# A fused attention, soft-MoE and SwiGLU kernel: the first SwiGLU units reordered, and weight conversion left out of iterations that end a pass

## The chip, the cores and the metric

One core of a Trainium2 chip runs the whole kernel. The time is device microseconds of one execution; of several executions the median is given. The engines are named as in the profile: PE (TensorE, matrix products; PEld is its weight load), DVE (VectorE), ACT (ScalarE), POOL (GpSimd), SP (SyncE, which issues the transfers here).

## The reference

Three layers follow each other on 4608 tokens of 512 features. The attention works in chunks of 64 tokens. The soft mixture of experts forms 32 slots from all tokens, sends each through its expert and mixes the slots back with a softmax `c` (one row of 32 weights for each token). The SwiGLU then is:

```python
g = x @ w_gate                    # w_gate, w_val: 512 x 1536, float64
silu = g * (1.0 / (1.0 + np.exp(-g)))
val = x @ w_val
out = (silu * val) @ w_out        # w_out: 1536 x 512, float64
```

The weights of the SwiGLU arrive as float64 and have to become float32 pairs on the chip.

## The kernel before, in words

**Stages.** Attention runs to about 128 us of the span, the experts to about 169 us, the SwiGLU from there to the end. Weights stream in through one queue (SP), in the order of the list `lq` (L128 to L138), as far as free slots of the pool `wp` allow.

**SwiGLU.** As `x` is `c` times the 32 slot outputs, the kernel multiplies the slot outputs with the gate and value weights first (`emit_g0` for chunk 0, L813; `emit_g` for the others, L822) and gets a small matrix `g_st`. For a block `b` of 512 tokens and a tile `f` of 128 hidden features, a unit (b, f), `emit_gv` (L840) makes two products with `c_t` (L847), ACT takes silu of one (L850), DVE multiplies by the other (L851). The unit's result is split into a high and a low float32r part: ACT copies (`hi`, L859), POOL or DVE subtracts (`lo`, L860). `emit_out` (L866) multiplies both with the high and low part of `w_out`: 4 tiles of 128 tokens by three products (L891 to L893; the first unit by L882), added up in PSUM over the units of a pass. At the end of a pass the four sums are copied out by ACT (L902) and DVE (L900), or added to the earlier sums by DVE (L904).

**Passes.** `SCHED` (L29) lists passes over 1536/256 = 6 weight chunks: blocks 0 to 4 with chunk 0 (two units each), then blocks 5 to 8 with chunks 0 and 1 (four units each), and so on; `seq` (L915) is the list of the 108 units, each with marks for the first and the last unit of its block's pass. Chunk 1 is used first by unit 12, (5, 2).

**Conversion.** Each half of a chunk of one weight kind ("g", "v", "o") goes through four stages: `conv_a` (ACT L185, DVE L186 and L187), `conv_b` (ACT L194, DVE L195), `conv_c` (DVE L200, POOL L213), `conv_d` (the high part by ACT L234, or by DVE L236 where asked; the low part L239 by POOL and DVE in turns). `conv_step` (L249) runs one stage of each half that is under way, last stage first, and starts a new half if told. Below, o01 is the second half of chunk 0 of `w_out`, v11 the second half of chunk 1 of `w_val`. The slot product of chunk 0 uses another form of conversion that ends at stage c.

**Order of issue.** The order on every engine is the order of these calls, written out by hand: L776 to L791 end the experts (`sos` L781, `sot_ps` L786, `so_t` L790 and L791), L921 to L939 issue the first two units and o00 and o01, and the loop over n (L949) issues, for each n:

- at its top, `conv_until`, which runs conversion steps until gate and value weights of unit n's chunk are done, and `emit_g` if that chunk has not had it;
- `emit_gv` of unit n, `emit_hl` (high and low part) of unit n-1;
- one `conv_step`, which may start a half if fewer than `RATE * n + R0` (0.38 n + 7.4) of the 36 halves are started;
- `emit_out` of unit n-2, and `emit_g` of the next chunk if its weights are done.

PSUM holds five tiles for the sums and the small slot products (`ps_o`), and three for L847 and the rest (`ps_g`).

Of the kernel before, what the change touches and what calls it, by code (L numbers as in the profile page):

```python
# [10 lines left out]
I32 = mybir.dt.int32  # L11
# [22 lines left out]
def tile_attn_softmoe_swiglu(  # L34
# [12 lines left out]
    nc = tc.nc  # L47
# [44 lines left out]
    def load_raw(kind, c, pool):  # L92
        src = {"o": w_out, "g": w_gate, "v": w_val}[kind][c]
        t = pool.tile([128, 2048], I32, tag="w", name="raw")
        nc.sync.dma_start(out=t, in_=src.bitcast(I32))
        raw_t[kind, c] = t[:, 0:1024], t[:, 1024:2048]

    raw0 = {}
# [169 lines left out]
    with tc.manual_schedule():  # L268
# [507 lines left out]
        dummy = sm.tile([128, 1], F32, tag="dm", name="dm", bufs=1)  # L776
        nc.scalar.activation(out=dummy, in_=cbias, func=ACTF.Silu)

        sos = t2.tile([128, DM], F32, tag="hs", name="sos", bufs=1)
        for o in range(0, DM, DM // 2):  # L780
            nc.scalar.activation(  # L781
# [3 lines left out]
        for kk in range(4):  # L785
            nc.tensor.matmul(  # L786
                out=sot_ps[kk // 2][:, kk % 2], lhsT=sos[:, kk * 128:(kk + 1) * 128],
                rhs=sel_big.rearrange("p j s -> p (j s)"), start=True, stop=True,
            )
        nc.scalar.activation(out=so_t[:, 0:2, 0:96], in_=sot_ps[0][:, :, 0:96], func=ACTF.Copy)  # L790
        nc.vector.tensor_copy(out=so_t[:, 2:4, 0:96], in_=sot_ps[1][:, :, 0:96])  # L791
        pp.close()
        pq.close()
        pa.close()
        ps_o = ctx.enter_context(tc.tile_pool(name="ps_o", bufs=5, space=PSUM, reuse_waits="tile"))
        ps_g = ctx.enter_context(tc.tile_pool(name="ps_g", bufs=3, space=PSUM, reuse_waits="tile"))
        ht2 = ctx.enter_context(tc.tile_pool(name="ht2", bufs=3, side="right"))
# [6 lines left out]
                out=so_hl[:, :, 96:128], in0=so_t[:, :, 0:32], in1=so_hl[:, :, 0:32].bitcast(F32), op=ALU.subtract  # L804
            )


        cvp[0] = ctx.enter_context(tc.tile_pool(name="cv2", bufs=4, side="right"))
        def evac_g(ps, gst):
            nc.scalar.activation(out=gst, in_=ps, func=ACTF.Copy)  # L810
            nc.vector.tensor_tensor(out=gst[64:96], in0=ps[64:96], in1=gst[64:96].bitcast(F32), op=ALU.subtract)
# [25 lines left out]
        def cols(parts):  # L837
            return [slice(i * 512 // parts, (i + 1) * 512 // parts) for i in range(parts)]

        def emit_gv(b, f, parts=1):  # L840
            c, ff = f // 2, (f % 2) * 128
            gp = ps_g.tile([128, 512], F32, tag="g", name="g_ps")
            vp = ps_g.tile([128, 512], F32, tag="g", name="v_ps")
            s = ht2.tile([128, 512], F32, tag="s", name="s_sb", bufs=2)
            for ps, gi in ((gp, 0), (vp, 1)):
                for k in cols(parts):
                    nc.tensor.matmul(out=ps[:, k], lhsT=g_st[:, c, gi, ff:ff + 128], rhs=c_blk(b)[:, k],  # L847
                                     start=True, stop=True)
            for k in cols(parts):
                nc.scalar.activation(out=s[:, k], in_=gp[:, k], func=ACTF.Silu)  # L850
                nc.vector.tensor_tensor(out=s[:, k], in0=s[:, k], in1=vp[:, k], op=ALU.mult)  # L851
            s_t[b, f] = s

        def emit_hl(b, f, eng, parts=1):
            s = s_t.pop((b, f))
            hi = ht2.tile([128, 512], F32R, tag="hi", name="hi_sb")
            lo = ht2.tile([128, 512], F32R, tag="lo", name="lo_sb")
            for k in cols(parts):
                nc.scalar.activation(out=hi[:, k], in_=s[:, k], func=ACTF.Copy)  # L859
                eng.tensor_tensor(out=lo[:, k], in0=s[:, k], in1=hi[:, k].bitcast(F32), op=ALU.subtract)  # L860
            hl[b, f] = (hi, lo)

        acc_t = {}
        part = {}

        def emit_out(b, f, first, last, mid=None):  # L866
            hi, lo = hl.pop((b, f))
            c, ff = f // 2, f % 2
            w = w_split("o", c)
            w_hi, w_lo = w[:, ff, 0], w[:, ff, 1]  # L870
            done = f == NFT - 1
            if last and not done and b not in part:
                assert slots[0]
                slots[0] -= 1
                resv[0] -= 1
                part[b] = wp.tile([128, 4, DM], F32, tag="w", name="part"), True
            if mid:
                for i, (x, w) in enumerate(((hi, w_hi), (lo, w_hi), (hi, w_lo))):
                    for t in range(4):
                        if i == 0:  # L880
                            acc_t[t] = ps_o.tile([128, DM], F32, tag="o", name=f"o{t}")
                        nc.tensor.matmul(out=acc_t[t], lhsT=x[:, t * 128:(t + 1) * 128], rhs=w, start=(i == 0), stop=False)  # L882
                    if i == 0:
                        mid()
                return
            for t in range(4):
                if first:
                    acc_t[t] = ps_o.tile([128, DM], F32, tag="o", name=f"o{t}")
                a = acc_t[t]
                ts = slice(t * 128, (t + 1) * 128)  # L890
                nc.tensor.matmul(out=a, lhsT=hi[:, ts], rhs=w_hi, start=first, stop=False)  # L891
                nc.tensor.matmul(out=a, lhsT=hi[:, ts], rhs=w_lo, start=False, stop=False)  # L892
                nc.tensor.matmul(out=a, lhsT=lo[:, ts], rhs=w_hi, start=False, stop=last)  # L893
                if not last:
                    continue
                p, new = part.get(b, (None, True))
                if True:
                    if new:
                        if t % 2:
                            nc.vector.tensor_copy(out=p[:, t], in_=a)  # L900
                        else:
                            nc.scalar.activation(out=p[:, t], in_=a, func=ACTF.Copy)  # L902
                    else:
                        nc.vector.tensor_tensor(out=p[:, t], in0=p[:, t], in1=a, op=ALU.add)  # L904
                if done:
                    r0 = b * 512 + t * 128
                    nc.sync.dma_start(out=out[r0:r0 + 128, :], in_=p[:, t])
            if last and b in part:
                part[b] = part[b][0], False
                if done:  # L910
                    del part[b]
                    slots[0] += 1
                    pump()

        seq = []  # L915
        for blocks, cs in SCHED:
            for b in blocks:
                fs = range(2 * cs[0], 2 * cs[-1] + 2)
                seq += [(b, f, f == fs[0], f == fs[-1]) for f in fs]
        gvs = [x[:2] for x in seq]  # L920
        conv_a()  # L921
        ev = [emit_g0(0, i, ps_g, "g") for i in range(2)]
        conv_a()
        ev[0]()
        conv_b()
        ev[1]()
        conv_c()
        emit_gv(*gvs[0], 2)
        conv_b()
        ev = [emit_g0(1, i, ps_o, "o") for i in range(2)]  # L930
        emit_hl(*gvs[0], nc.vector, 2)
        conv_d()
        ev[0]()
        ev[1]()
        conv_c()
        emit_so_hl()
        emit_out(*seq[0], lambda: emit_gv(*gvs[1], 2))
        conv_d(nc.gpsimd, nc.vector)
        emit_hl(*gvs[1], nc.vector, 2)  # L939
        g_done = [1]  # L940

        def try_g():
# [6 lines left out]
        for n in range(len(seq) + LAG):  # L949
# [5 lines left out]
            if 1 < n < len(seq):  # L955
                emit_gv(*gvs[n])
            if 2 < n <= len(seq):
                emit_hl(*gvs[n - 1], nc.vector if n < 3 else nc.gpsimd)
            if 1 <= n < len(seq):
                conv_step(36 - len(conv_q) < RATE * n + R0)  # L960
            if n > LAG:
                f = seq[n - LAG][1]
# [56 lines left out]
```

## Time and profile before

| what | value |
|---|---|
| median of 3 runs | 544.61 us (543.85 to 545.26) |
| the profiled execution's own time | 543.5 us |
| its span, first to last instruction | 541.7 us |
| PE busy | 521.3 us, 96% of the span |
| DVE busy | 406.7 us, 75% |
| ACT busy | 260.4 us, 48% |
| POOL busy | 252.9 us, 47% |
| mean granted PE clock | 0.996 |

The span is what the rows below count from; the execution's time is 1.8 us longer than it. A timeline row gives start, duration, engine, line, operation, tile written and tiles read, shape, count, and in brackets the engine's idle time just before it and what ended it. Busy time of PE is modelled for its pipelined products: products that follow each other start about 0.23 us apart at 512 columns and are drawn 0.39 us long.

### The profile page before, as it was taken

To read this page: it belongs to the slowest core of one execution; us is meant where nothing else is said; L and a number is where in the kernel's file an instruction comes from. 1 tells how busy PE (TensorE), PEld (TensorE's weight loads), DVE (VectorE), ACT (ScalarE), POOL (GpSimd) and SP (SyncE) were. 2 spreads that over 40 slices of the span, in tenths; PEclk is the share of its full clock that TensorE was granted. 3 is DMA by queue.
4 is the path that set the end of the run, shared out by engine and by line. 5 is a ranking of instruction groups with operands and counts; after the bars stand their busy time and mean duration, and the time that the engine had idled before them with its cause. 6 is when DMAs were issued, how large, how long until landed. Compare 5 with 4: busy or idle time off the path is not lost.

```text
span 541.7 us, 11039 instructions
## 1 busy us (share of the span) xinstructions
PE 521.3 (96%) x4389; PEld 409.8 (76%) x4389; DVE 406.7 (75%) x673; ACT 260.4 (48%) x504; POOL 252.9 (47%) x252
## 2 busy tenths in 40 slices
PE   7899999998998889999999999999999999999997
PEld 6778887873335568888888888888888888888885
DVE  5778987864766999888898889989898943433554
ACT  1344533342447766666565555545654533333331
POOL 3333343321002576576566756656664743343342
PEclk9999999999999989999999999999999999999999
DMA  8999999999999502020202220222000000222344
GB/s 324 404 358 398 348 405 347 413 416 400 421 416 417 247 1 77 2 78 2 77 1 77 77 79 0 79 79 77 0 1 0 3 0 1 77 79 77 113 179 174
DMA packets 23762, 91.09 MB, mean 168 GB/s; under 512 B 3104, under 2 KB 3104, under 8 KB 17696
## 3 DMA queue, kind: packets, MB, share of 16 engines
q1 hardware_dynamic: 23712, 90.40, 43.1%
q8 instruction: 34, 0.56, 0.4%
q14 instruction: 16, 0.13, 0.1%
HBM read 80.95 MB, written 9.44 MB: 167 GB/s over the span
## 4 chain that ended last, share of the span: by engine, by line
PE 81%; DVE 9%; DMA 6%; issue 2%; ACT 1%; POOL 0%; SPq 0%; ACTq 0%; DVEq 0%
PE o L891 18%; PE o L893 18%; PE o L892 18%; DMA w2t<-in_moe_w_dram 6%; PE v_ps L847 4%; PE g_ps L847 4%; PE xa_ps L365 4%; PE xt_ps L401 3%; PE s_ps L328 3%; PE pt_ps L351 2%; PE gg_ps L828 2%; PE si_ps L484 1%; DVE ssb L338 1%; DVE m L336 1%; PE h_ps L652 1%
## 5 line engine op out<-in xcount | busy, mean ns | idle before, releaser
L860 POOL TENSOR_TENSOR lo_sb<-s_sb,hi_sb 128x512 fp32r<-128x512 f32 x106 | 140.5, 1326 | 130.9 <-ACT hi_sb L859 127.9
L891 PE MATMUL o<-whl,hi_sb 128*128 128x512 f32 x428 | 167.7, 392 | 2.5 <-DVE part L900 2.5
L893 PE MATMUL o<-whl,lo_sb 128*128 128x512 f32 x428 | 167.2, 391 | 0.5 <-POOL lo_sb L860 0.5
L892 PE MATMUL o<-whl,hi_sb 128*128 128x512 f32 x428 | 167.1, 390 | 0.0
L850 ACT ACTIVATE s_sb<-g_ps 128x512 f32<-128x512 f32 (+1 forms) x110 | 64.7, 590 | 149.9 <-PE g_ps L847 147.7
L851 DVE TENSOR_TENSOR s_sb<-s_sb,v_ps 128x512 f32<-128x512 f32 (+1 forms) x110 | 74.0, 674 | 74.5 <-ACT s_sb L850 73.2
L891 PEld LDWEIGHTS o<-whl,hi_sb 128*128 128x128 f32 x428 | 80.6, 188 | 22.2 <-DVE part L900 4.5
L893 PEld LDWEIGHTS o<-whl,lo_sb 128*128 128x128 f32 x428 | 80.6, 188 | 17.8 <-POOL lo_sb L860 0.9
L892 PEld LDWEIGHTS o<-whl,hi_sb 128*128 128x128 f32 x428 | 80.6, 188 | 16.3
L859 ACT ACTIVATE hi_sb<-s_sb 128x512 fp32r<-128x512 f32 (+1 forms) x110 | 67.6, 616 | 0.8 <-DVE s_sb L851 0.8
L904 DVE TENSOR_TENSOR part<-part,o 128x512 f32<-128x512 f32 x92 | 57.1, 677 | 2.6 <-PE o L893 2.6
L318 POOL COPY vbd<-vbd 64x520 f32<-64x520 f32 x36 | 22.3, 619 | 69.9 <-DMA vbd<-in_v_dram 56.2
L213 POOL TENSOR_TENSOR mt<-mt,ex 128x512 f32<-128x512 f32 x32 | 39.5, 1234 | 27.5 <-PE g_ps L847 13.8
L200 DVE SCALAR_TENSOR_TENSOR ex<-raw,ex 128x512 uint16<-128x512 uint16 x32 | 47.2, 1477 | 0.1
L847 PE MATMUL v_ps<-c_t,g_st 128*128 128x512 f32 (+1 forms) x110 | 42.5, 390 | 0.8 <-DMA raw<-in_moe_w_val_dram 0.5
L847 PE MATMUL g_ps<-c_t,g_st 128*128 128x512 f32 (+1 forms) x110 | 42.4, 389 | 0.1
L353 ACT ACTIVATE pt<-pt_ps 128x512 f32<-128x512 f32 x36 | 19.5, 596 | 36.2 <-PE pt_ps L351 36.2
L195 DVE SCALAR_TENSOR_TENSOR mt<-mt,raw 128x512 f32<-128x512 f32 x32 | 34.9, 1090 | 0.0
L336 DVE TENSOR_REDUCE m<-s_ps 128x16 f32<-128x1024 f32 x18 | 22.0, 1224 | 14.8 <-PE s_ps L328 14.7
L187 DVE TENSOR_SCALAR mt<-raw 128x512 int32<-128x512 int32 x32 | 32.9, 1027 | 0.0
L365 PE MATMUL xa_ps<-vbd,pt 128*64 128x130 f32 x432 | 28.2, 277 | 0.0
L403 ACT ACTIVATE xt<-xt_ps 128x512 f32<-128x512 f32 (+1 forms) x36 | 19.3, 596 | 13.7 <-PE xt_ps L401 10.2
(138 smaller groups left out, 664.2 us busy)
## 6 DMA issues: line engine op xcount, KB each, us to landing
qk<-in_qk_dram SPq DMA_DIRECT2D x36, 512.0 KB, 6.6
w1t<-in_moe_w_dram SPq DMA_DIRECT2D x16, 1024.0 KB, 9.3
w2t<-in_moe_w_dram SPq DMA_DIRECT2D x15, 1024.0 KB, 13.5
vbd<-in_v_dram SPq DMA_DIRECT2D x36, 260.0 KB, 7.5
out_dram<-part SPq DMA_DIRECT2D x36, 256.0 KB, 2.2
raw<-in_moe_w_out_dram SPq DMA_DIRECT2D x6, 1024.0 KB, 7.1
raw<-in_moe_w_gate_dram SPq DMA_DIRECT2D x5, 1024.0 KB, 4.8
raw<-in_moe_w_val_dram SPq DMA_DIRECT2D x5, 1024.0 KB, 5.1
```

The lines of the kernel that those rows point to most:

```text
L200: nc.vector.scalar_tensor_tensor(out=ex, in0=hh, scalar=0x8000, in1=ex, op0=ALU.bitwise_and, op1=ALU.bitwise_or)
L213: nc.gpsimd.tensor_tensor(out=m, in0=m, in1=p, op=ALU.mult)
L365: nc.tensor.matmul(out=banks[n // 3][64 * cc:64 * cc + 64, (n % 3) * 2 * VW:(n % 3 + 1) * 2 * VW], lhsT=pt_t[i][:, j, 64 * cc:64 * cc + 64 ...
L847: nc.tensor.matmul(out=ps[:, k], lhsT=g_st[:, c, gi, ff:ff + 128], rhs=c_blk(b)[:, k], start=True, stop=True)
L850: nc.scalar.activation(out=s[:, k], in_=gp[:, k], func=ACTF.Silu)
L851: nc.vector.tensor_tensor(out=s[:, k], in0=s[:, k], in1=vp[:, k], op=ALU.mult)
L859: nc.scalar.activation(out=hi[:, k], in_=s[:, k], func=ACTF.Copy)
L860: eng.tensor_tensor(out=lo[:, k], in0=s[:, k], in1=hi[:, k].bitcast(F32), op=ALU.subtract)
L891: nc.tensor.matmul(out=a, lhsT=hi[:, ts], rhs=w_hi, start=first, stop=False)
L892: nc.tensor.matmul(out=a, lhsT=hi[:, ts], rhs=w_lo, start=False, stop=False)
L893: nc.tensor.matmul(out=a, lhsT=lo[:, ts], rhs=w_hi, start=False, stop=last)
L904: nc.vector.tensor_tensor(out=p[:, t], in0=p[:, t], in1=a, op=ALU.add)
```

## The change

Five edits. (1) The first chunk of `w_out` arrives in two transfers of 512 KB. (2) The pool of the conversion is opened before `sos`, and o00's `conv_a` is issued ahead of the copies of `so_t`. (3) The hand-written beginning has another order: the second slot product (`emit_g0(1, ..)`) is issued inside and behind the first unit's two products, o01 goes through its stages after o00, o00's high part is copied by DVE and o01's by ACT, the first unit's high part, o00's last stage and o01's first stage come before the first unit's low part, and `emit_so_hl` comes last. (4) Unit 0's products take high by high, high by low, low by high (the last two changed places). (5) In the loop, no `conv_step` is issued where `emit_out` of that iteration ends a pass; `conv_until` is as before.

```diff
@@ load_raw
-        nc.sync.dma_start(out=t, in_=src.bitcast(I32))
+        step = 1024 if (kind, c) == ("o", 0) else 2048
+        for o in range(0, 2048, step):
+            nc.sync.dma_start(out=t[:, o:o + step], in_=src.bitcast(I32)[:, o:o + step])
@@ end of the experts
+        pa.close()
+        cvp[0] = ctx.enter_context(tc.tile_pool(name="cv2", bufs=4, side="right"))
         sos = t2.tile([128, DM], F32, tag="hs", name="sos", bufs=1)
...
+        conv_a()
         nc.scalar.activation(out=so_t[:, 0:2, 0:96], in_=sot_ps[0][:, :, 0:96], func=ACTF.Copy)
         nc.vector.tensor_copy(out=so_t[:, 2:4, 0:96], in_=sot_ps[1][:, :, 0:96])
         pp.close()
         pq.close()
-        pa.close()
@@ emit_gv
                     nc.tensor.matmul(out=ps[:, k], lhsT=g_st[:, c, gi, ff:ff + 128], rhs=c_blk(b)[:, k],
                                      start=True, stop=True)
+                if mid and gi == 0:
+                    mid()
@@ emit_hl becomes emit_hi (all of L859), then emit_lo (all of L860)
@@ emit_out, first unit
-                for i, (x, w) in enumerate(((hi, w_hi), (lo, w_hi), (hi, w_lo))):
+                for i, (x, w) in enumerate(((hi, w_hi), (hi, w_lo), (lo, w_hi))):
@@ the beginning
-        conv_a()
-        ev = [emit_g0(0, i, ps_g, "g") for i in range(2)]
-        conv_a()
-        ev[0]()
-        conv_b()
-        ev[1]()
-        conv_c()
-        emit_gv(*gvs[0], 2)
-        conv_b()
-        ev = [emit_g0(1, i, ps_o, "o") for i in range(2)]
-        emit_hl(*gvs[0], nc.vector, 2)
-        conv_d()
-        ev[0]()
-        ev[1]()
-        conv_c()
-        emit_so_hl()
-        emit_out(*seq[0], lambda: emit_gv(*gvs[1], 2))
-        conv_d(nc.gpsimd, nc.vector)
-        emit_hl(*gvs[1], nc.vector, 2)
+        ev = [emit_g0(0, i, ps_g, "g") for i in range(2)]
+        conv_b()
+        ev[0]()
+        conv_c()
+        ev[1]()
+        ev = []
+        emit_gv(*gvs[0], 2, lambda: ev.append(emit_g0(1, 0, ps_o, "o")))
+        ev.append(emit_g0(1, 1, ps_o, "o"))
+        ev[0]()
+        emit_hi(*gvs[0], 2)
+        conv_d(nc.gpsimd, nc.vector)
+        conv_a()
+        ev[1]()
+        emit_lo(*gvs[0], nc.vector, 2)
+        conv_b()
+        conv_c()
+        emit_out(*seq[0], lambda: emit_gv(*gvs[1], 2))
+        emit_hi(*gvs[1], 2)
+        emit_lo(*gvs[1], nc.vector, 2)
+        conv_d(nc.gpsimd)
+        emit_so_hl()
@@ the loop
-            if 1 <= n < len(seq):
+            if 1 <= n < len(seq) and not (n > LAG and seq[n - LAG][3]):
                 conv_step(36 - len(conv_q) < RATE * n + R0)
```

## Rows read from the trace of the kernel before

**Rows 1.** Waits of PE from 168 us to the end: total, times, longest.
```profile
PE o L891 <- DVE part L900: 2.5, 1, 2.5
PE o L882 <- DVE g_st L811: 1.0, 1, 1.0
...
PE v_ps L847 <- ACT s_sb L850: 0.3, 1, 0.3
```

**Rows 2.** Windows: length, busy PE, PEld, DVE, ACT, POOL, granted clock, DMA share, GB/s.
```profile
184.00:219.00 35.00, 31.96 (x138) 25.41 (x138) 32.72 (x43) 25.04 (x45) 22.78 (x17) 0.95 0.09 34
192.10:195.60 3.50, 3.46 (x9) 2.69 (x10) 3.06 (x5) 1.17 (x3) 2.15 (x3) 0.54 0.02 5
260.00:360.00 100.00, 100.00 (x456) 82.92 (x456) 88.54 (x113) 55.94 (x98) 63.42 (x48) 1.00 0.15 53
```

**Rows 3.** Timeline of PE around its longest wait.
```profile
192.14 0.63 PE L891 MATMUL o<-whl,hi_sb 128*128 128x512 f32 x1 [2.53 <-DVE part L900]
...
195.55 0.49 PE L891 MATMUL o<-whl,hi_sb 128*128 128x512 f32 x1
195.88 0.39 PE L892 MATMUL o<-whl,hi_sb 128*128 128x512 f32 x1
```

**Rows 4.** Timelines of DVE and POOL ahead of that wait's end.
```profile
186.65 1.52 DVE L200 SCALAR_TENSOR_TENSOR ex<-raw,ex 128x512 uint16<-128x512 uint16 x1
...
189.75 1.45 POOL L860 TENSOR_TENSOR lo_sb<-s_sb,hi_sb 128x512 fp32r<-128x512 f32 x1
189.99 1.49 DVE L187 TENSOR_SCALAR mt<-raw 128x512 int32<-128x512 int32 x1
...
191.40 1.28 DVE L900 COPY part<-o 128x512 f32<-128x512 f32 x2
```

**Rows 5.** Transfers by line, issues of two short windows, with times to landing.
```profile
L89 SPq DMA_DIRECT2D w2t<-in_moe_w_dram x2: 328/328/328, 150.8 to 153.2; - x2
DMA to landing us min/median/max: 15.5/16.1/16.7
...
L95 SPq DMA_DIRECT2D raw<-in_moe_w_out_dram x1: 328/328/328, 155.8 to 155.8; - x1
DMA to landing us min/median/max: 15.4/15.4/15.4
```

**Rows 6.** Timeline of all engines at the beginning of the SwiGLU.
```profile
170.82 0.33 ACT L790 ACTIVATE so_t<-sot_ps 128x192 f32<-128x192 f32 x1 [0.44 <-PE sot_ps L786]
171.23 1.25 ACT L185 ACTIVATE raw<-raw 128x512 f32<-128x512 uint32 x2
...
176.60 0.63 ACT L234 ACTIVATE whl<-mt 128x512 fp32r<-128x512 f32 x1 [0.27 <-POOL mt L213]
...
177.28 0.98 PE L882 MATMUL o<-whl,hi_sb 128*128 128x512 f32 x3 [0.56 <-ACT whl L234]
177.45 0.52 ACT L802 ACTIVATE so_hl<-so_t 128x384 fp32r<-128x384 f32 x1
178.90 0.49 DVE L811 TENSOR_TENSOR g_st<-gg_ps,g_st 32x128 fp32r<-32x128 f32 x2
...
179.43 0.69 DVE L200 SCALAR_TENSOR_TENSOR ex<-raw,ex 128x512 uint16<-128x512 uint16 x1
...
180.20 1.17 POOL L213 TENSOR_TENSOR mt<-mt,ex 128x512 f32<-128x512 f32 x1 [1.61 <-DVE ex L200]
...
182.37 0.60 ACT L850 ACTIVATE s_sb<-g_ps 128x512 f32<-128x512 f32 x1 [0.17 <-PE g_ps L847]
183.02 0.50 PE L847 MATMUL v_ps<-c_t,g_st 128*128 128x512 f32 x1 [0.30 <-ACT s_sb L850]
```

**Rows 7.** Timeline around the slot product of chunk 1, and unit 12's first product.
```profile
207.65 2.07 PE L828 MATMUL gg_ps<-whl,so_hl 128*128 128x256 f32 x16
...
209.75 0.60 ACT L810 ACTIVATE g_st<-gg_ps 128x512 fp32r<-128x512 f32 x1 [2.57 <-PE gg_ps L828]
210.38 0.69 DVE L811 TENSOR_TENSOR g_st<-gg_ps,g_st 32x512 fp32r<-32x512 f32 x1 [1.20 <-ACT g_st L810]
...
219.10 0.39 PE L847 MATMUL g_ps<-c_t,g_st 128*128 128x512 f32 x1
```

More of the change, by code (lines that the diff above doesn't have):

```diff
@@ L805, in emit_so_hl @@
             )
-        cvp[0] = ctx.enter_context(tc.tile_pool(name="cv2", bufs=4, side="right"))
         def evac_g(ps, gst):
@@ L838, in cols, with emit_gv @@
             return [slice(i * 512 // parts, (i + 1) * 512 // parts) for i in range(parts)]
-        def emit_gv(b, f, parts=1):
+        def emit_gv(b, f, parts=1, mid=None):
             c, ff = f // 2, (f % 2) * 128
@@ L852, in emit_gv, with emit_hi, emit_lo, emit_hl @@
             s_t[b, f] = s
-        def emit_hl(b, f, eng, parts=1):
-            s = s_t.pop((b, f))
+        def emit_hi(b, f, parts=1):
             hi = ht2.tile([128, 512], F32R, tag="hi", name="hi_sb")
+            for k in cols(parts):
+                nc.scalar.activation(out=hi[:, k], in_=s_t[b, f][:, k], func=ACTF.Copy)
+            hl[b, f] = hi
+        def emit_lo(b, f, eng, parts=1):
+            s, hi = s_t.pop((b, f)), hl[b, f]
             lo = ht2.tile([128, 512], F32R, tag="lo", name="lo_sb")
             for k in cols(parts):
-                nc.scalar.activation(out=hi[:, k], in_=s[:, k], func=ACTF.Copy)
                 eng.tensor_tensor(out=lo[:, k], in0=s[:, k], in1=hi[:, k].bitcast(F32), op=ALU.subtract)
             hl[b, f] = (hi, lo)
+        def emit_hl(b, f, eng):
+            emit_hi(b, f)
+            emit_lo(b, f, eng)
         acc_t = {}
@@ L957, in tile_attn_softmoe_swiglu @@
             if 2 < n <= len(seq):
-                emit_hl(*gvs[n - 1], nc.vector if n < 3 else nc.gpsimd)
-            if 1 <= n < len(seq):
+                emit_hl(*gvs[n - 1], nc.gpsimd)
+            if 1 <= n < len(seq) and not (n > LAG and seq[n - LAG][3]):
                 conv_step(36 - len(conv_q) < RATE * n + R0)
```

## The prediction, made before the changed kernel ran

> **What bounds the kernel now.** I read PE's waits first [rows 1], then the engines' busy time by stretch [rows 2]. From the SwiGLU's start the list of PE's waits has eight entries; the longest is 2.5 us, all eight lie before 193 us, and from 260 to 360 us PE is busy 100.00 us of 100.00 at clock 1.00. So PE's products set the end, and a microsecond gained or lost before about 220 us goes through to the end, unless a new wait eats it. The case is decided between 170 and 220 us.
>
> In that stretch PE is not alone: from 184 to 219 us DVE is busy 32.72 us of 35.00 [rows 2], so it has 2.3 us to spare. The longest wait shows why. PE waits 2.53 us until 192.14 for a PSUM sum that DVE copies out by L900 [rows 3], and L900 comes at 191.40, behind four conversion operations of DVE, from L200 at 186.65 to L187 at 189.99 [rows 4]. These are slow because POOL works: L200 takes 1.52 us there, 0.69 us at 179.43 [rows 4, 6]; L187's 1.49 us ends with POOL's L860 in between [rows 4]. I read the rows as one of the two going at a time. After the wait the granted clock is 0.54 [rows 2], between PE's 1.2 and 2.4 GHz levels: the nine products from 192.14 to 195.55 start 0.43 us apart (3.41 us for eight steps), while a step takes 0.23 us later. That is 3.4 - 1.8 = 1.6 us lost, so wait and clock together cost 4.1 us.
>
> **How I worked.** I wrote down the order of issue of each engine before and after, up to unit 12, and walked the queues with the rows' durations: an operation starts when its engine is free and its inputs are there, and POOL and a DVE operation on SBUF alone take turns. Walked for the old order this gives unit 12's first product at 219.7 us, the row says 219.10 [rows 7]; the walk is 0.6 us late, and I take that off below.
>
> **The transfer.** Two halves of 512 KB of the last expert weights were issued at 150.8 and 153.2 us and landed 16.7 and 15.5 us later, at 167.5 and 168.7. The first `w_out` chunk, issued at 155.8, landed at 171.2 [rows 5]. So the queue is full and halves land 1.2 us apart: o00's half should land at 169.9, o01's at 171.2. One more issue of 0.33 us on SP moves all later loads one place back; with 15 us between issue and landing that costs nothing. The Trainium skill (DMA: Bandwidth & Descriptors, section Bandwidth) speaks against the split: transfers should be 1 MiB or more to reach 75% of peak. By that rule the half would come late, perhaps with the whole; the row of two 512 KB halves at the full queue's rate does not bear it out here.
>
> **The beginning.** ACT has 0.44 us idle before L790, and L185 takes 0.62 us (1.25 for two) [rows 6]: `so_t` comes 0.1 us later, 0.8 us later if the half lands with the whole. Moving the second slot product forward takes away PE's 1.0 us wait of unit 0's fourth sum [rows 1], as its PSUM tile is read early, and o00's high part no longer follows ACT's other copies: unit 0's products start at about 176.6 instead of 177.28 [rows 6] and end 0.8 us earlier. (Bounds: 0 and 1.5.) But see what now stands on ACT ahead of unit 2's silu: unit 1's high part, L234 of o01, L802, L185 of g10. L234 needs POOL's L213 of o01, which needs DVE's L200, and on DVE that follows the second L811 (which now sits behind L187 while POOL does o00's low part), the first unit's low part and L195. Counted: L811 done 178.6; low parts 0.7, L195 0.6, L200 0.6 give 180.5; L213 1.2, L234 0.6, L802 0.5, L185 0.6 give about 183.5; silu 0.6 more. Unit 3's second product, which needs that PSUM tile, then starts at 184.1 instead of 183.02 [rows 6]: the beginning is 1.1 us later in the end, and PE's wait there grows from 0.3 to about 2.5 us. (Bounds: 0.8 earlier; 1.1 later and, as the clock fell after 2.53 us, 1.6 more.) I take +1.1. The swap of low and high products costs nothing, both parts being there in time.
>
> **The left-out steps.** Iteration 3 ends a pass; without its step DVE copies out directly. The 2.5 us and the 1.6 us of clock go: -4.1, net -3.0 at unit 5.
>
> What is left out has to come later. Steps now run at n = 1, 2, 4, 6, 8, 10. By the rate rule halves start at n = 1, 2, 4, 6 (g10, g11, v10, v11; before at 1, 2, 3, 5), and v11 needs three more steps: 8, 10 and the next. Before, its last stage came at n = 8, `emit_g` ran behind that iteration at 207.65, and its result was used eleven microseconds later, at 219.10 [rows 7]. Now v11 is unfinished when n = 12 begins; `conv_until` forces its last stage there, PE meets `emit_g` directly, and directly behind it unit 12's product, which needs its result.
>
> The price of this: the steps at 6, 8 and 10 carry up to four stages each, and POOL's and DVE's turns fill up; low parts of units 6 and 8 arrive late by about 1.5 us together (bounds 0 and 2.8). So PE meets `emit_g` at 217.2 - 3.0 + 1.5 = 215.7 us, where 217.2 is 219.10 less the 1.9 us that `emit_g` takes PE in its old place (2.07 with the drawn end of its last product) [rows 7]. It does 13 of 16 products in 1.6 us, the next needs v11's low part (DVE L239). DVE, meanwhile, is at unit 10's multiplication until 212.8, and before that L239 come L200 of v11, L195 of o10, L186 and L187 of o11, each beside a POOL operation (0.9, 1.9, 1.5, 1.5: the sizes of [rows 4]), unit 11's multiplication 0.6, two L900 1.2, then L239 0.6: 221.0. PE waits 3.6 us. Then three products 0.4, L810 0.6, L811 0.7 [rows 7] and the gaps between engines: unit 12 starts at 223.1, 4.0 us later than before; less the walk's 0.6 us, +3.4. The clock, which fell after 2.53 us idle, probably falls after 3.6; half of such a stretch passes in the wait for L811, so +0.8. Bounds of the wait at unit 12: 1.7 us (all inputs ready, only L810 and L811 in the way) to 5.4.
>
> From unit 12 on chunks 2 to 5 are converted three or more iterations before use, by the same count; nothing changes there. Only o21 gets close (last stage at n = 30, used at 31): 0, at most 1.5.
>
> **Sum:** +1.1 - 4.1 + 1.5 + the rest of the wait at unit 12 = +3.4, +0.8 clock: +4.2 us. Against the profiled execution's own 543.5 us that is 547.7. That execution lies 1.1 us under the median of the three runs, 544.61, so for the median I forecast 548.8 us.
>
> **Rivals.**
>
> 1. DVE keeps up (faster). With L900 no longer behind a conversion, DVE and POOL use their idle time, the beginning comes out even (0), v11's low part is there before PE is 13 products into `emit_g`, and only 1.7 us of L810 and L811 remain: -4.1 + 1.7 = -2.4, 542.2 us. It decides where DVE's L239 of v11 starts. For it: 2.3 us idle. Against it: 93% busy, and the same operations have to be done 3 us earlier. Chance 0.20.
>
> 2. It evens out: the wait at unit 12 is 3 to 4 us, without a fall of the clock: about 544.6, within 1.6 us. Chance 0.16.
>
> 3. Worse: the wait of 2.5 us in the beginning also takes the clock, or o21 comes late: +6 to +7, 551. Chance 0.10.
>
> 4. The first half does not land early, as the rule on transfer sizes would have it: `so_t` and all behind it 0.7 us later, 549.5. Chance 0.06.
>
> The forecast itself, 547.2 to 550.5, has 0.48. About 0.3% (1.6 us) is what a measurement of this kernel can tell from no change. Faster by more than that is rival 1 (0.20), the same is rival 2 (0.16), slower is the forecast and rivals 3 and 4 (0.64). The range reaches from rival 1's middle to rival 3's, 542.4 to 551.2; some 0.1 of rival 1 and as much of rival 3 stay outside.
>
> **What would show it.** Right: the 2.5 us wait for L900 is gone; PE's waits have new entries for L828 on v11's `whl` (about 3.6 us) and for L847 on L811 (about 1.6 us) near 216 to 223 us, and L847 on L850's silu (about 2.5 us) near 184. The clock is under 1.00 in the stretch behind 221 us. From 230 us on PE has no wait. Wrong: `emit_g` of chunk 1 runs without a wait, or unit 12 starts before 219 us. The first step is wrong if ACT's L185 before L790 waits for a transfer until 171 us.

## The result, and the profile after

The changed kernel takes 551.58 us (median of 6 runs, 549.83 to 553.39); the kernel before, on the same chip, 544.93 us (6 runs, 543.31 to 545.69). The ratio is 1.0113, 95% interval 1.0080 to 1.0146: slower by 6.6 us, in the forecast direction, 0.4 us beyond the top of the range. As a change it stands at the range's top, which is +6.6 us (551.2 less the 544.6 that the forecast counted from).

The profiled execution took 553.24 us, its span is 551.5 us, the mean granted clock 0.988. Lines have moved: L185 is L187 now, L186/L187 are L188/L189, L195 L197, L200 L202, L234/L236/L239 L236/L238/L241, L810/L811 L812/L813, L828 L830, L847 L849, L850 L854, L860 L868, L891 to L893 L903 to L905, L900 L912.

**First a correction that all comparisons below need.** 3.0 us of the 9.8 us between the two spans lie ahead of everything that the change touches. Windows of the unchanged code between attention and experts, with the columns of [rows 2]; first after, then before:

```profile
120.00:130.00 10.00, 8.03 (x94) 4.02 (x96) 4.73 (x17) 4.11 (x15) 1.53 (x5) 0.82 1.01 418
130.00:140.00 10.00, 9.66 (x74) 4.34 (x70) 4.68 (x23) 1.22 (x5) 0.43 (x3) 0.84 0.65 242
```

```profile
120.00:130.00 10.00, 7.97 (x105) 4.67 (x101) 5.30 (x20) 4.19 (x15) 1.53 (x5) 1.00 1.01 417
130.00:140.00 10.00, 9.66 (x85) 3.34 (x88) 5.57 (x29) 3.01 (x7) 0.65 (x5) 1.00 1.00 398
```

In this execution of the changed kernel the granted clock fell there (0.82 and 0.84 over ten microseconds each), in that of the kernel before it did not. Among the experiments' profiled executions it fell there in e2, e7 and e9, two of which are near copies of the kernel before. The attention too ends up to 3.5 us earlier or later from one execution to the next (the first product of L508 there, L506 in the kernel before and its near copies, starts at 125.7 us before, at 126.3 after, at 129.2 in e4). So I count from the first slot product (L786, now L790), which starts at 170.07 us before and at 173.07 us after. From there to the end of the span it is 371.6 us before and 378.4 us after: **+6.8 us**, close to the medians' 6.65. I call it the SwiGLU stretch.

PE's waits from the SwiGLU's start to the end, to be held against [rows 1]:

```profile
PE gg_ps L830 <- DVE whl L241: 2.5, 1, 2.5
PE v_ps L849 <- ACT s_sb L854: 2.1, 1, 2.1
PE g_ps L849 <- DVE g_st L813: 1.4, 1, 1.4
PE o L894 <- DVE whl L238: 0.9, 1, 0.9
...
PE o L904 <- DVE whl L241: 0.6, 1, 0.6
...
PE o L905 <- POOL lo_sb L868: 0.6, 2, 0.4
PE o L903 <- DVE part L912: 0.6, 2, 0.3
```

The wait of 2.5 us for a sum copied out by DVE is gone (L912, 0.3 at most now), as the left-out step at n = 3 was to do. Three waits of 1.4 to 2.5 us stand in its place. On PE's timeline they are these; the first row is the beginning, the next three are `emit_g` of chunk 1 and unit 12's first product (which was at 219.10 in [rows 7]), the last is o21's:

```profile
186.91 0.50 PE L849 MATMUL v_ps<-c_t,g_st 128*128 128x512 f32 x1 [2.07 <-ACT s_sb L854]
...
219.14 1.71 PE L830 MATMUL gg_ps<-whl,so_hl 128*128 128x256 f32 x13
223.31 0.63 PE L830 MATMUL gg_ps<-whl,so_hl 128*128 128x256 f32 x3 [2.46 <-DVE whl L241]
225.34 0.79 PE L849 MATMUL g_ps<-c_t,g_st 128*128 128x512 f32 x1 [1.41 <-DVE g_st L813]
...
290.91 0.50 PE L904 MATMUL o<-whl,hi_sb 128*128 128x512 f32 x1 [0.64 <-DVE whl L241]
```

What DVE does while PE waits at unit 12 (DVE's timeline):

```profile
215.53 0.88 DVE L202 SCALAR_TENSOR_TENSOR ex<-raw,ex 128x512 uint16<-128x512 uint16 x1
216.33 1.78 DVE L197 SCALAR_TENSOR_TENSOR mt<-mt,raw 128x512 f32<-128x512 f32 x1
218.04 1.38 DVE L188 TENSOR_SCALAR ex<-raw 128x512 uint16<-128x512 uint16 x1
219.34 1.52 DVE L189 TENSOR_SCALAR mt<-raw 128x512 int32<-128x512 int32 x1
220.78 0.67 DVE L855 TENSOR_TENSOR s_sb<-s_sb,v_ps 128x512 f32<-128x512 f32 x1
221.38 1.27 DVE L912 COPY part<-o 128x512 f32<-128x512 f32 x2
222.58 0.68 DVE L241 TENSOR_TENSOR whl<-mt,whl 128x512 fp32r<-128x512 f32 x1
```

This is the queue that the prediction walked, operation by operation: v11's third stage, o10's second, two operations of o11's first, a multiplication, two copies, and only then the low part of v11 that PE's fourteenth product needs.

The windows, with the columns of [rows 2]:

```profile
184.00:219.00 35.00, 31.95 (x128) 24.41 (x127) 33.01 (x42) 25.87 (x47) 22.31 (x16) 0.95 0.10 40
187.50:191.00 3.50, 3.50 (x10) 2.74 (x9) 3.17 (x7) 2.71 (x6) 1.28 (x1) 0.54 0.06 23
225.30:228.80 3.50, 3.46 (x8) 2.78 (x9) 1.29 (x2) 1.64 (x3) 1.49 (x2) 0.51 0.00 0
260.00:360.00 100.00, 99.18 (x449) 81.43 (x448) 87.78 (x110) 56.00 (x99) 64.16 (x48) 1.00 0.14 48
```

DVE is no less loaded than before from 184 to 219 us (33.01 of 35.00 us against 32.72; from 187 to 222 us, the same place counted from the first slot product, it is 33.65). In the SwiGLU the clock falls twice now, behind the wait for the silu and behind those at unit 12, each time at 0.51 to 0.54 for about 3.5 us; before it fell once. And from 260 to 360 us PE is idle for 0.8 us, where it was for none.

**Where the time goes, unit by unit.** The start of each unit's first product (`g_ps`) against the kernel before, both counted from the first slot product, in us. The last column is the end of the span. Kernels e1 to e11 are the experiments below.

| kernel | unit 6 | 11 | 12 | 13 | 31 | 57 | 107 | end |
|---|---|---|---|---|---|---|---|---|
| after | -2.8 | -3.0 | +3.2 | +5.0 | +4.4 | +6.3 | +6.7 | +6.8 |
| e1: left-out steps alone | -4.5 | -4.4 | +1.8 | +3.5 | +2.9 | +4.9 | +5.3 | +5.3 |
| e2: beginning alone | -1.2 | +0.4 | +0.4 | +0.4 | +0.4 | +0.4 | +0.4 | +0.5 |
| e3: steps left out only before unit 12 | -4.1 | -4.1 | +2.1 | +3.6 | +3.6 | +3.6 | +3.7 | +3.7 |
| e4: steps left out only after unit 12 | +0.3 | +0.3 | +0.3 | +0.3 | -0.2 | +1.0 | +1.5 | +1.5 |
| e5: steps of n = 9 and 11 given back | -4.1 | -1.1 | -1.1 | -1.1 | -1.6 | +0.3 | +0.7 | +0.8 |
| e6: kernel before, no steps at 3, 5, 7 | -4.4 | -1.5 | -1.4 | -1.4 | -1.4 | -1.4 | -1.3 | -1.3 |
| e11: o11 not started at n = 10 | -4.2 | -4.1 | -0.2 | +1.5 | +7.1 | +9.0 | +9.5 | +9.6 |

A jump between two columns is a loss at that place. (Up to unit 11 the kernel before has paid for `emit_g` of chunk 1, some 2 us [rows 7], and the kernels that do it late have not.) After shows four things: it is ahead at unit 6, then comes a loss of 6.2 us between units 11 and 12, 1.7 us more to unit 13, and 2.3 us between units 31 and 107.

### The profile page after: what moved, and what is told of

Its sections match the earlier page's. It is cut to its first block, busy times and chain, and to the rows that moved or that the text cites. A ratio compares the mean times of both kernels' runs of the same rounds, so it can differ in the third digit from the quotient of the medians.

```text
span 551.5 us, 11044 instructions
## 1 busy us (share of the span) xinstructions
PE 530.1 (96%) x4389; PEld 415.3 (75%) x4389; DVE 407.2 (74%) x673; ACT 259.0 (47%) x504; POOL 258.9 (47%) x252
## 4 chain that ended last, share of the span: by engine, by line
PE 83%; DVE 8%; issue 2%; ACT 2%; POOL 2%; DMA 1%; SPq 0%; ACTq 0%; DVEq 0%; POOLq 0%
PE o L905 16%; PE o L904 16%; PE o L903 16%; PE xa_ps L367 4%; PE g_ps L849 4%; PE v_ps L849 4%; PE xt_ps L403 3%; PE s_ps L330 3%; PE pt_ps L353 3%; PE so_ps L697 3%; PE h_ps L654 3%; PE si_ps L486 2%; PE gg_ps L830 2%; PE xb_ps L367 1%; PE lt_ps L422 1%
## 5 line engine op out<-in xcount | busy, mean ns | idle before, releaser
L868 POOL TENSOR_TENSOR lo_sb<-s_sb,hi_sb 128x512 fp32r<-128x512 f32 x106 | 141.0, 1331 | 130.3 <-ACT hi_sb L861 128.0
L905 PE MATMUL o<-whl,lo_sb 128*128 128x512 f32 x428 | 168.4, 394 | 0.6 <-POOL lo_sb L868 0.6
L903 PE MATMUL o<-whl,hi_sb 128*128 128x512 f32 x428 | 168.2, 393 | 0.6 <-DVE part L912 0.6
L904 PE MATMUL o<-whl,hi_sb 128*128 128x512 f32 x428 | 167.8, 392 | 0.6 <-DVE whl L241 0.6
L854 ACT ACTIVATE s_sb<-g_ps 128x512 f32<-128x512 f32 (+1 forms) x110 | 64.8, 591 | 144.8 <-PE g_ps L849 126.8
L855 DVE TENSOR_TENSOR s_sb<-s_sb,v_ps 128x512 f32<-128x512 f32 (+1 forms) x110 | 73.9, 674 | 70.2 <-ACT s_sb L854 67.4
L905 PEld LDWEIGHTS o<-whl,lo_sb 128*128 128x128 f32 x428 | 81.0, 189 | 20.2 <-POOL lo_sb L868 3.5
L903 PEld LDWEIGHTS o<-whl,hi_sb 128*128 128x128 f32 x428 | 81.1, 190 | 18.5 <-DVE part L912 1.7
L904 PEld LDWEIGHTS o<-whl,hi_sb 128*128 128x128 f32 x428 | 81.1, 189 | 17.9 <-DVE whl L241 0.9
L215 POOL TENSOR_TENSOR mt<-mt,ex 128x512 f32<-128x512 f32 x32 | 43.4, 1355 | 27.7 <-DVE ex L202 13.7
L849 PE MATMUL v_ps<-c_t,g_st 128*128 128x512 f32 (+1 forms) x110 | 42.6, 390 | 2.7 <-ACT s_sb L854 2.1
L849 PE MATMUL g_ps<-c_t,g_st 128*128 128x512 f32 (+1 forms) x110 | 42.7, 391 | 1.4 <-DVE g_st L813 1.4
L202 DVE SCALAR_TENSOR_TENSOR ex<-raw,ex 128x512 uint16<-128x512 uint16 x32 | 39.7, 1241 | 0.0
L189 DVE TENSOR_SCALAR mt<-raw 128x512 int32<-128x512 int32 x32 | 34.1, 1066 | 0.0
L197 DVE SCALAR_TENSOR_TENSOR mt<-mt,raw 128x512 f32<-128x512 f32 x32 | 33.6, 1049 | 0.1
L241 POOL TENSOR_TENSOR whl<-mt,whl 128x512 fp32r<-128x512 f32 x17 | 27.1, 1595 | 2.2 <-DVE whl L238 1.4
```

Of the source, the lines that this page charges most:

```text
L202: nc.vector.scalar_tensor_tensor(out=ex, in0=hh, scalar=0x8000, in1=ex, op0=ALU.bitwise_and, op1=ALU.bitwise_or)
L215: nc.gpsimd.tensor_tensor(out=m, in0=m, in1=p, op=ALU.mult)
```

## Experiments

### Which part of the change costs (e1 to e4)

e1 is the kernel before with the rule of edit 5 alone:

```diff
-            if 1 <= n < len(seq):
+            if 1 <= n < len(seq) and not (n > LAG and seq[n - LAG][3]):
```

> The old beginning with the new rule alone: no conversion step in iterations that end a pass. Theory A (the left-out steps make the gate and value weights of chunk 1 late for unit 12, so PE waits there and the clock falls): slower than before by 3 to 5 us, with PE waiting on L239's whl and then on L811's g_st, 3.5 to 5 us together, near unit 12; the 2.5 us wait on L900 is gone. Rival B (the reordered beginning is what costs, the left-out steps are a gain of 4 us): faster than before by 2 to 4 us.

e2 is the changed kernel without that rule (edits 1 to 4 alone):

```diff
-            if 1 <= n < len(seq) and not (n > LAG and seq[n - LAG][3]):
+            if 1 <= n < len(seq):
```

> The new beginning alone, with a conversion step in every iteration as before. Theory A: 0.5 to 2 us slower than before (unit 3's second product waits about 2 us for ACT's silu; the wait for L900 in iteration 4 stays, shorter), no wait at unit 12. Rival B: slower than before by 5 us or more, close to the changed kernel.

e3 is the changed kernel with the rule only up to unit 12:

```diff
-            if 1 <= n < len(seq) and not (n > LAG and seq[n - LAG][3]):
+            if 1 <= n < len(seq) and not (LAG < n < 12 and seq[n - LAG][3]):
```

> The changed kernel, but steps are left out in the first pass only (n below 12). Theory A, with the part that the waits near 290, 344 and 395 us (2 us together) come from steps left out later: 1 to 2.5 us faster than the changed kernel, those later waits gone, the waits at unit 12 as in the changed kernel. Rival C (the later waits come with the delayed conversion whatever happens later, or are not on the path): the time of the changed kernel within 0.7 us.

e4 is the changed kernel with the rule only behind unit 12:

```diff
-            if 1 <= n < len(seq) and not (n > LAG and seq[n - LAG][3]):
+            if 1 <= n < len(seq) and not (n > 12 and seq[n - LAG][3]):
```

> The changed kernel, but steps are left out only behind the first pass (n above 12). Theory A: 4 to 6 us faster than the changed kernel, no wait at unit 12, the later waits still there, so 1 to 2.5 us slower than the new beginning alone. Rival C: the time of the new beginning alone within 0.7 us.

| kernel | median, us | kernel before, us | ratio (95%) |
|---|---|---|---|
| e1 | 550.40 | 545.07 | 1.0084 (1.0054 to 1.0113) |
| e2 | 545.25 | 545.07 | 1.0004 (0.9980 to 1.0029) |
| e3 | 550.43 | 545.07 | 1.0094 (1.0064 to 1.0125) |
| e4 | 547.37 | 545.07 | 1.0034 (1.0000 to 1.0068) |

The left-out steps alone make the kernel slower; the beginning alone changes nothing that can be measured. Within the rule the five steps that are left out before unit 12, at n = 3, 5, 7, 9 and 11, do most of it, and those behind unit 12 cost a little (e4's interval begins at 1). Two sizes missed the expectation: e1's 5.3 us are more than 3 to 5, e2's 0.2 less than 0.5 to 2. In the table by units e3 loses all that it loses between units 11 and 13 and stays at +3.6 or +3.7 to the end, and e4 is about level up to unit 31 and then loses: the losses sit where the steps are missing (units 11 to 13: after 7.9 us, e3 7.7; units 31 to 107: after 2.3, e4 1.7).

e1's waits of PE show the pattern of after on the old beginning: the 2.5 us wait for L900 is gone (0.3 at most), and this has come:

```profile
PE gg_ps L828 <- DVE whl L239: 2.4, 1, 2.4
PE g_ps L847 <- DVE g_st L811: 1.4, 1, 1.4
...
PE o L892 <- DVE whl L239: 0.6, 1, 0.6
...
PE v_ps L847 <- ACT s_sb L850: 0.3, 1, 0.3
```

The wait for the silu stays at 0.3 us there: that one belongs to the new beginning, and e2 to e4, which have the new beginning, show 2.1 us.

### The two sides of the left-out steps (e5, e6)

e5 is the changed kernel with the steps of iterations 9 and 11 issued again, so that v11 is through before unit 12:

```diff
-            if 1 <= n < len(seq) and not (n > LAG and seq[n - LAG][3]):
+            if 1 <= n < len(seq) and not (n > LAG and n not in (9, 11) and seq[n - LAG][3]):
```

> The changed kernel with the conversion steps of iterations 9 and 11 put back, so that chunk 1's last gate or value half is finished in iteration 10 and not at the top of 12. Theory A: the waits for L241's whl and L813's g_st near unit 12 (2.5 and 1.4 us) and the clock's fall behind them go, some of it returns as waits for DVE's copies; 3 to 5.5 us faster than the changed kernel. Rival D (DVE and POOL are simply full until unit 12, so that the same time is waited for somewhere else): within 1.5 us of the changed kernel.

545.88 us, ratio 1.0024 (0.9990 to 1.0058) to the kernel before (545.17 us beside it). Of PE's list the waits for L241 and L813 at unit 12 are gone, and unit 13 is at -1.1 us. Against e3, whose clock also held in the beginning, that is 4.7 us from two steps. What stays against the kernel before is the loss behind unit 31, which e5 shares with after, e1 and e4.

e6 gives the kernel before only the useful part of the rule:

```diff
-            if 1 <= n < len(seq):
+            if 1 <= n < len(seq) and n not in (3, 5, 7):
```

> The old beginning, steps left out in iterations 3, 5 and 7 only. Theory A: the wait for L900 and its clock loss (4.1 us) go and chunk 1 is in time, so faster than before, by 1 to 4 us. Rival D: DVE and POOL have no room, the wait moves to low parts or to copies between 195 and 222 us: within 1 us of before.

545.19 us against 545.17, ratio 0.9995 (0.9972 to 1.0018), as Rival D had it. In the profiled execution the stretch is 1.3 us shorter and the clock falls nowhere in it while PE works, but the medians don't show a gain. At unit 6 it leads by 4.4 us: that is the wait and the clock, 4.1 us by the prediction. By unit 11 only 1.5 us are left. The window says why; DVE is busy 34.58 of 35.00 us:

```profile
184.00:219.00 35.00, 32.57 (x145) 25.29 (x144) 34.58 (x45) 25.34 (x46) 23.64 (x17) 1.00 0.11 39
```

and PE has these waits in place of the long one:

```profile
PE o L891 <- DVE part L900: 1.5, 2, 1.2
...
PE o L893 <- POOL lo_sb L860: 0.9, 2, 0.5
```

I read this as the work of DVE and POOL together being the limit up to unit 12; e7 and e12, further down, try it. Leaving steps out moves their operations; it doesn't take any away.

### What PE waits for at unit 12 (e11)

The changed kernel, with no half started at n = 10, which takes o11's first operations out of DVE's queue ahead of v11's low part:

```diff
-                conv_step(36 - len(conv_q) < RATE * n + R0)
+                conv_step(n != 10 and 36 - len(conv_q) < RATE * n + R0)
```

> The changed kernel, but iteration 10 starts no half, so that o11's L188 and L189 (1.4 and 1.5 us beside POOL) no longer stand on DVE ahead of L241 of v11. Theory A, with the DVE queue as the cause of the wait: the wait on L241's whl near unit 12 falls from 2.5 to under 0.7 us, the one on L813's g_st (1.4 us) stays, no or a shorter fall of the clock there; 2 to 4 us faster than the changed kernel. If instead the forced step at the top of iteration 12 is late by itself (its place, not what stands ahead): the wait stays over 1.8 us, the time within 1 us of the changed kernel.

551.69 us against 544.36, ratio 1.0118 (1.0074 to 1.0163): no gain at all, where I had expected 2 to 4 us. But the place that it was to tell about came out. PE runs all 16 products of `emit_g` without a wait, only that for L813 is left, and the loss between units 11 and 12 falls from 6.2 to 3.9 us. Against e3, whose clock held in the beginning as well, unit 12 comes 2.3 us earlier, the whole of that wait. On DVE's timeline nothing of o11 stands ahead of L241 any more:

```profile
212.11 1.78 DVE L197 SCALAR_TENSOR_TENSOR mt<-mt,raw 128x512 f32<-128x512 f32 x1
213.81 0.67 DVE L855 TENSOR_TENSOR s_sb<-s_sb,v_ps 128x512 f32<-128x512 f32 x1
214.41 1.40 DVE L912 COPY part<-o 128x512 f32<-128x512 f32 x2
215.73 0.99 DVE L241 TENSOR_TENSOR whl<-mt,whl 128x512 fp32r<-128x512 f32 x1
```

The clock is another miss: I had expected no fall or a shorter one, and it falls behind the 1.41 us for L813 alone (0.53 from 219.4 to 222.9 us). Then PE stands a little later, at unit 13's output products, for o11 itself (PE's timeline):

```profile
214.92 2.47 PE L830 MATMUL gg_ps<-whl,so_hl 128*128 128x256 f32 x16
218.80 0.50 PE L849 MATMUL g_ps<-c_t,g_st 128*128 128x512 f32 x1 [1.41 <-DVE g_st L813]
...
232.74 0.49 PE L903 MATMUL o<-whl,hi_sb 128*128 128x512 f32 x1 [2.07 <-ACT whl L236]
233.86 0.79 PE L904 MATMUL o<-whl,hi_sb 128*128 128x512 f32 x1 [0.62 <-DVE whl L241]
```

and the clock is down behind that too, for twice as long as behind the waits in after:

```profile
232.70:239.50 6.80, 6.14 (x14) 4.64 (x15) 2.92 (x4) 1.25 (x3) 1.72 (x2) 0.54 0.28 117
```

That what stands ahead of L241 on DVE causes the 2.5 us wait is thereby shown, and so is that postponing o11 doesn't cure it: o11 is due right behind v11.

### The transfer in two halves (e8)

The changed kernel with the first `w_out` chunk in one transfer, all else as changed:

```diff
-        step = 1024 if (kind, c) == ("o", 0) else 2048
+        step = 2048
```

> The changed kernel with the first output chunk in one transfer again. If the half really lands 1.2 us earlier and L187 (old L185) stands ahead of the copy of so_t: so_t 0.7 to 1.0 us later, the start of unit 0's products later by as much, at most 1 us slower than the changed kernel in all. If the split does nothing: the same within 0.3 us, ACT's first L187 at the same distance from sos.

552.46 us against 545.17, ratio 1.0135 (1.0107 to 1.0163). The stretch is 379.2 us, 0.8 us longer than after's, and lags by 0.8 us at units 6, 12 and 13 alike. ACT's first row shows where it starts; the copy of `so_t`, right behind it on ACT, is late by as much, and PE's list has a new wait for it (ACT's timeline, then PE's waits):

```profile
172.90 0.67 ACT L187 ACTIVATE raw<-raw 128x512 f32<-128x512 uint32 x1 [0.66 <-DMA raw<-in_moe_w_out_dram]
173.47 0.31 ACT L795 ACTIVATE so_t<-sot_ps 128x192 f32<-128x192 f32 x1
```

```profile
PE gg_ps L819 <- ACT so_t L795: 0.7, 1, 0.7
```

The new order, where o00's conversion stands ahead of `so_t`, needs the split, and the split gives it these 0.8 us. That rests on the two profiles; the intervals of the two kernels overlap (after's is 1.0080 to 1.0146).

### Less work for DVE instead of later work (e7, e9, e10, e12)

If DVE and POOL are the limit up to unit 12, a step must be taken off them. e7 is the kernel before, with all four sums of chunk 0's passes copied out by ACT (L902) instead of two by DVE (L900):

```diff
-                        if t % 2:
+                        if t % 2 and c:
```

> The kernel before, with all four copies at the end of a first-pass block on ACT, none on DVE (5 times 1.27 us less on DVE before unit 12). If DVE's load up to unit 12 is what PE waits for (both theories' root): the wait of 2.5 us for a copy shrinks to under 1 us and the clock does not fall there, 1.5 to 4 us faster than before. If DVE's load does not matter as such, only the order: within 1 us of before.

543.14 us against 545.17, ratio 0.9975 (0.9948 to 1.0001). The stretch is 1.2 us shorter. PE waits for no copy any more and the clock doesn't fall there; but four waits for low parts from POOL have come, 2.7 us in all:

```profile
PE o L893 <- POOL lo_sb L860: 2.7, 4, 1.0
```

The Trainium skill (Perfetto Trace Analysis, section Optimizing Scalar/DVE Operations) says that moving some work to ScalarE may make sense where DVE is saturated, and that moves between GpSimd and DVE might not help. e7 goes with the first (1.2 us of stretch, though its interval just reaches 1). e12 tries the second on top of e7: three low parts from POOL to DVE.

```diff
-                        if t % 2:
+                        if t % 2 and c:
...
-                emit_hl(*gvs[n - 1], nc.vector if n < 3 else nc.gpsimd)
+                emit_hl(*gvs[n - 1], nc.vector if n in (5, 7, 9) else nc.gpsimd)
```

> A version meant to beat both: the kernel before with the first-pass copies on ACT, and the low parts issued in iterations 5, 7 and 9 on DVE instead of POOL, since with the copies on ACT alone PE's only waits in the pass are for POOL's low parts (2.7 us in four). If POOL's queue is what is left: the waits for low parts fall from 2.7 to 1 to 2 us, and it is 0.5 to 1.5 us faster than with the copies alone, 1.5 to 4 us faster than before. Rival: DVE, loaded again, takes the gain back: within 0.5 us of the version with the copies alone.

543.09 us against 544.21, ratio 0.9976 (0.9959 to 0.9993). The waits for low parts shrink from 2.7 to 2.0 us, one for ACT's copy comes:

```profile
PE o L893 <- POOL lo_sb L860: 1.6, 3, 0.6
...
PE o L891 <- ACT part L902: 0.7, 1, 0.7
...
PE o L893 <- DVE lo_sb L860: 0.4, 1, 0.4
```

The stretch is 0.3 us shorter than e7's, less than these runs can tell apart; so the rival of this expectation came true. e12 and e7 are the fastest kernels of the study (ratios 0.9976 and 0.9975). e12 is 1.1 us under the kernel before in the medians and 1.5 us in the stretch: small, but its interval lies under 1.

Starting halves later over the whole kernel was to spare the front as well. e9 is e7 with a smaller constant in the rate rule, e10 the kernel before with that and no step at n = 3:

```diff
-R0 = 7.4
+R0 = 6.9
```

> A version meant to beat both: the old beginning, first-pass copies on ACT, and the start rule's R0 at 6.9 instead of 7.4 (halves start 1.3 iterations later). If DVE's and POOL's load up to unit 12 is the limit, starting chunk 1's output halves later takes two of POOL's operations out of the way of the low parts: 0.5 to 1.5 us faster than with the copies on ACT alone, 2 to 4 us faster than before. Rival: chunk 1 comes late again, PE waits at unit 12.

> The old beginning with R0 at 6.9 and no step in iteration 3 alone; copies as before. One left-out step where the 2.5 us wait was, and fewer halves under way before unit 12. If the load is the limit: 1 to 4 us faster than before, the wait for L900 under 1.3 us and no fall of the clock in the first pass. Rival: the left-out step makes v11 late, PE waits at unit 12, within 1 us of before or slower.

e9: 546.03 us against 544.36, ratio 1.0009 (0.9983 to 1.0034). e10: 546.41 us, ratio 1.0026 (0.9996 to 1.0056). Neither helps. Neither has the waits of unit 12 that the rivals had; e10's longest wait for L900 is 1.5 us, where I had expected less than 1.3. e9 is 2.0 us ahead at unit 13, more than e7, and 0.3 us behind at unit 107. Both lose behind unit 31, where three waits for DVE's adding-up of sums (L904) come:

```profile
PE o L891 <- DVE part L904: 1.5, 3, 0.6
```

That row is e9's; e10's is the same with 0.5 as the longest. In e10's profile the clock fell in the beginning as well, see the last section. The late loss is like that of the rule's later left-out steps (e4). I take it that what is taken from the front meets the next passes, where DVE is loaded as well (87.78 of 100.00 us from 260 to 360, in after).

## Why the prediction was right, and where it was short

The direction, the place and the chain of causes came as forecast; the size was +6.6 us instead of +4.2. Step by step, counted from the first slot product:

- **The transfer: right.** The half was issued at 159.2 us, landed 13.8 us later, at 173.0, and its conversion ran when the slot products did. From the first slot product, that is -0.1 us (forecast -0.2), against +1.1 us for the whole before [rows 5, 6] and +1.0 us in e8. `so_t` on ACT starts 0.77 us behind the first slot product, before 0.75 us: no cost, as the 0.1 us said. The Trainium skill's rule (DMA: Bandwidth & Descriptors, section Bandwidth), of 1 MiB or more for 75% of peak, is not borne out here: the half landed 1.1 us ahead of where the whole does in e8. e8's 0.8 us is what rival 4's 0.7 us would have been.
- **The beginning: mechanism right, the clock left out of the sum.** Unit 0's products start 6.50 us behind the first slot product, before 7.21: 0.7 us earlier, as forecast. They end 1.1 us earlier, I had 0.8. Then ACT's silu is late behind o01's high part, L806 and L187, as counted. PE's wait for it is 2.07 us (2.5 forecast), and the product behind it comes 13.84 us after the first slot product, before 12.95: +0.9 us, forecast +1.1. By unit 13 hardly anything of that is left where the clock holds (e3 +3.6 against e1's +3.5). But in this execution the clock fell, and after stands at +5.0 where e3 has +3.6. Of the 1.6 us that I had as an upper bound and in rival 3, 1.3 came.
- **The left-out step at n = 3: right.** 2.5 us of wait and 1.6 us of clock gone, 4.1 us forecast; e1, which has this alone, leads by 4.5 us at unit 6.
- **Late low parts: about right.** From unit 8 to unit 11 the lead goes from -2.8 to -3.0 us, while the kernel before spends some 2 us on `emit_g`; so nearly 2 us are lost there, forecast 1.5. PE meets `emit_g` 0.4 us later than forecast (219.14 less the 3.0 us of the front is 216.1, forecast 215.7).
- **Unit 12: right in kind, shorter in wait.** DVE's queue is the one walked, with the durations forecast (0.88, 1.78, 1.38 and 1.52 us beside POOL; forecast 0.9, 1.9, 1.5, 1.5). I called these "the sizes of [rows 4]", but those rows have only 1.52 us for L200 and 1.49 for L187; the 0.9 and the 1.9 don't stand there. L241 ends at 220.3 in before's time, forecast 221.0; with PE's later arrival the wait is 2.46 us instead of 3.6. L813 adds 1.41 (1.6 forecast). Unit 12 starts +3.2 us late, forecast +3.4. That these agree so well is partly luck: the clock's fall in the beginning is in the 3.2 and not in the 3.4; without it e3 is at +2.1 and e1 at +1.8.
- **The clock behind unit 12: mis-sized.** I took half of a stretch, 0.8 us, because the wait for L813 falls into it. The rows behind unit 12 show 0.51 over 3.5 us of products, and from unit 12 to 13 after loses 1.7 us, e1 1.7, e3 1.5. The whole price was to be paid.
- **Later: wrong.** "Nothing changes there", I wrote of the units behind 12, and took o21 at 0, at most 1.5. From unit 31 to 107 after loses 2.3 us, e1 2.4, e5 2.4, e4 1.7, all with later steps left out, and e2, e3 and e6, without, lose 0.1 at most. In after 1.05 us of it come at unit 32, with o21, whose low part PE waits for at 290.91. Nearly all of the rest comes where PE waits for POOL's low part (L868), at 319.93, 344.36, 348.01 and 394.83 us. Each time an operation of the conversion (L215) stands just ahead of that low part on POOL, as here (POOL's timeline, then PE's):

```profile
345.54 1.17 POOL L215 TENSOR_TENSOR mt<-mt,ex 128x512 f32<-128x512 f32 x1 [1.23 <-ACT hi_sb L861]
346.66 1.29 POOL L868 TENSOR_TENSOR lo_sb<-s_sb,hi_sb 128x512 fp32r<-128x512 f32 x1
```

```profile
348.01 0.50 PE L905 MATMUL o<-whl,lo_sb 128*128 128x512 f32 x1 [0.18 <-POOL lo_sb L868]
```

  The failed step is that I counted when halves are due, and not what the moved steps stand ahead of in the queues of the iterations they move into; here that is mostly POOL's.

The sum by the rows: +3.2 at unit 12, +1.7 clock, +1.8 later (the 2.3 us less 0.5 us that the later left-out steps gain between units 13 and 31: after, e1, e4 and e5 have this gain, e2, e3 and e6 have not), which makes 6.7 of the 6.8 us. Of the rivals the first (DVE keeps up) is refuted by DVE's timeline, and the second by the clock. What came is rather rival 3, "the wait of 2.5 us in the beginning also takes the clock, or o21 comes late: +6 to +7", in both its halves on top of the forecast; I gave it 0.10 because I took its parts for unlikely one by one, though the wait of 2.5 us that I forecast there was as long as the one that had taken the clock before.

The size of the clock's part is a matter of the execution: the six executions of the changed kernel have mean granted clocks of 0.986 to 0.997 with spans of 551.6 to 548.0 us. So the median of a kernel above can differ from its profiled stretch by a fall or by the attention's spread, as e3's does (+5.4 us in the median, +3.7 in the stretch).

## What to carry to other kernels

Where two engines are full, leaving work out of one iteration is only moving it: look for the first consumer that has a due time behind the gap, and write down the engine's queue in front of it; here two steps decided nearly 5 us. A wait of PE is priced with the clock's fall that may come behind it, also for waits that a change newly makes, and a wait that is removed buys only what the next limit (here DVE and POOL up to unit 12) leaves of it. What helped a little (1.2 to 1.5 us of stretch) was to give the loaded engine less to do (two copies per pass to ACT), not to let it do it later.

## What was not expected of the hardware

- **A fall of the clock in code that nobody touched.** Between 120 and 140 us the granted clock is 0.81 to 0.85 in four of the fourteen profiled executions (after, e2, e7, e9), and 1.00 in the others. From L508's first product to the first slot product it is 46.8 us in after, with the fall, and 43.9 us in e1 and e3, without: 2.9 us. What starts it I have not found: PE's idle times just ahead, 1.02 and 0.76 us, are the same in after and in e3.
- **The same wait with and without a fall.** PE waits 2.06 to 2.08 us for the silu in the beginning in all kernels with the new one. Behind it the clock is at 0.54 in after and e2 and at 0.56 in e8, over 3.5 us, and at 1.00 in e3, e4, e5 and e11. Of e3 (first) and e2 the windows right behind the wait:

```profile
184.50:188.00 3.50, 3.50 (x17) 2.79 (x15) 3.50 (x8) 3.26 (x6) 1.13 (x1) 1.00 0.08 33
```

```profile
188.00:191.50 3.50, 3.50 (x10) 2.77 (x9) 3.50 (x7) 3.50 (x7) 1.29 (x1) 0.54 0.06 26
```

  17 products start in the one, 10 in the other. What decides it is not shown. After and e2 are the ones of the seven whose clock had fallen at 126 us as well, and e8 alone has the 0.7 us wait for `so_t`; but e10 has neither, and there the clock falls in the old beginning, behind the 1.0 us wait of unit 0's fourth sum [rows 1], which before, e1, e6, e7, e9 and e12 have without a fall. It is at 0.51 from 181.5 to 185.0 us, and unit 2 is 1.6 us late. As long as nothing tells the cases apart, such a fall can be priced only as a chance: behind the silu's wait three in seven by these executions.
- **DVE and POOL take turns on SBUF, and some of DVE's operations are exempt.** L189 takes 0.41 us at 187.17, with POOL idle, and 1.52 us at 219.34 beside POOL; L855, which reads PSUM, takes 0.67 us at 187.51, with POOL idle, and 0.67 us at 207.80, inside POOL's L868. The Trainium skill (SBUF — State Buffer, section SBUF: two separate sides) calls the port that the two share an exclusive lock, held for a whole instruction; the rows agree. It makes POOL's idle time no reserve while DVE works on SBUF, and DVE's 33.01 of 35.00 us partly waiting.
